# Routed attention and a SoLU expert: six early exponentials stored in the place of w_in, a new sharing of the first casts and marks, a later first v load, and a new order of the early work

## The chip, the cores and the metric

The kernel runs on one core of a Trainium2 chip. A core has five instruction queues that run side by side: TensorE (PE, matrix multiplication, with its weight loads shown apart as PEld), VectorE (DVE), ScalarE (ACT), GpSimd (POOL) and SyncE (SP, which here only issues DMA transfers). Data live in SBUF, matmul results in PSUM banks of 512 float32 columns. Each queue runs its instructions in order and waits where one needs something of another queue. The metric is the time of one execution on the device in microseconds; a profile records one execution, with the span from its first to its last instruction.

## What is computed

Sizes: batch 4, 8 heads, 768 tokens, 64 columns per head, 16 cluster centroids per head; model width 512, inner width 1024.

```python
q_n, k_n, c_n = q / (|q| + 1e-6), k / (|k| + 1e-6), centroids / (|centroids| + 1e-6)
q_assign = argmax(q_n @ c_n.T)          # cluster of every query, per head
k_assign = argmax(k_n @ c_n.T)          # cluster of every key
mask = q_assign[:, None] == k_assign[None, :]
scores = where(mask, (q @ k.T) / 8, -1e9)
attn = softmax(scores) @ v
x = attn, heads side by side            # 3072 tokens x 512
h = x @ w_in                            # 3072 x 1024
solu = h * softmax(h)
out = layer_norm(solu) * g_ln @ w_out   # 3072 x 512
```

## The kernel before

**The mask in the matmul.** A head's 64 columns of q and k are extended by 16 rows that hold, for each token, a one at its own cluster (a "mark"; 32 rows where two heads share a transfer). One matmul over 80 or 96 rows then gives the score plus a constant where the clusters agree, and the exponential of the scaled and shifted result is near zero elsewhere. So the tiles `qk` (six of them, used in turn, one per pair of heads) get their first 64 rows from casts and the rest from the marks.

**The stages of one pair of heads.** The names are those of the order strings; a name such as `ca0.0.1.0.1` has batch, pair, 0 for q or 1 for k, head of the pair, and for pair 0 of batch 0 the half of the tokens.

- `ld` loads q and k into `raw`, `lv` loads v into `vf` (L528), both issued by SP, in order. At most eight transfers are in flight, since a transfer uses one of eight semaphores in turn and waits for the one before it there. The first half-loads are issued partly from ScalarE's queue.
- Batch 0 is turned on TensorE (`tp`, L387) into one of three banks of `hreg`, and copied out as float32 `xt` (`xa`, L394) by VectorE or ScalarE. The other batches are turned on VectorE (`xt`, L408).
- `ca` casts a head's half of `xt` to bfloat16 in `qk` (L432 on ScalarE, L434 and L436 elsewhere).
- `cl` multiplies `xt` with the normalised centroids (L451, L446); VectorE turns the result back (`tb`, L460), takes the largest of each 16 (`mx`, L473), compares (`oh`, L485 or L479), and turns the marks (`ot`, L495 or L492). `pl` places them in `qk` (L515, or L507 for pairs 1 to 3 of batch 0), `bl` clears 16 rows (L524).
- `S` are the score matmuls (L602) into one of three PSUM banks `sps`; `E` the exponentials on ScalarE (L608) into one of nine SBUF tiles `e`; `V` multiplies them with v and a column of ones (L625; v cast by `cv`, L533); `N` divides by the sum (L637, L650).

Pair 0 of batch 0 works with halves of 384 tokens: its two heads have units 0 to 3 of six score banks each, 128x384. All later units have three banks of 512 columns. An `S` waits for the `E` three banks back, an `E` for the `V` that read the tile nine banks back.

**The expert.** `li` and `lo` load w_in and w_out, `wi` casts w_in into `w_in_sb` (L553), `su`, `sk`, `me`, `ce` take the mean out of w_out (L575 to L588). For each of 24 token tiles x is turned by a DMA (`tx`, L680), then `h` (L711), its maximum `hm` (L717), exponential `ex` (L723), product `u` (L730), turned by a DMA (`tu`, L735), statistics `bn`, `ag`, `at`, `al`, the second product `y` (L775), scaling `sc` (L790 or L792) and output `ou` (L802).

**What sets the order.** Everything is added to a list with what it needs, and five strings `ORDER`, written out by hand or by a search, give each engine's queue by these short names with counts (`S2 tp` is two score banks and one turn). `AWAY` names the operations that run on another engine than the usual one. `wm` and `fl` are idle matmuls at the start (L820). Before the loads of w_in are cast, part of `w_in_sb` holds the identity's index (`idx_i`, the first 256 of its first 1024 columns) and the normalised centroids (`c_n`, 256 columns of the second 1024).

Of the kernel before, what the change touches and what calls it, by code (L numbers as in the profile page):

```python
# [22 lines left out]
class Weave:  # L23
# [6 lines left out]
        ld4 lv si ld4 lv lg ld4 lv2 ld4 lo2 ld4 lo ld3 lo ld3 li4 tx ld3 lv3 tx ld4 tu ld9 lv ld tu  # L30
        tx ld3 tu ld3 ou ld2 ou ld tu ld12 tu ld4 lv ld2 ou tx ld3 tu ou ld2 tx lv ld tu ld4 tx ld
        tu ou2 ld lv ld4 tu ld4 tu ld ou ld7 pl ou ld lv2 ld3 tu lv tx ou tu lv pl ld4 ou2 tx lv tu
        tx ou tu pl2 tu2 tx tu tx ou2 tx ou tu tx2 ou tu2 ou2 tu2 ou6
    """
    ORDER["POOL"] = """
        po z ca2 pl2 cv z bl pl2 ca z ca pl2 ca z2 ca3 cv ca cv ca pl3 sg ca cv2 pl3 ca2 gs pl ca cv
        ca wi ca pl2 wi3 bl ca pl2 cv at cv pl ca pl al bl at cv ca pl ca pl cv ca3 al at ca al ca
        at ca pl2 bl cv pl2 ca4 at ca2 al ca pl2 bl pl2 cv2 ca3 al at pl2 bl pl2 ca pl al ca3 at cv
        at pl ca pl2 ca2 pl al cv2 bl cv2 pl2 ca pl al pl at al at pl2 ca3 at al bl cv pl2 bl cv2
        ca3 pl5 al cv3 at al ca2 cv ca cv ca2 at ca2 pl ca al pl2 at2 pl3 at ca cv al at2 al2 at2 al  # L40
        at al3 at al2 at2 al2
    """
    ORDER["PE"] = """
        wm tp2 cp tp cl tp fl5 cl fl4 S3 tp2 S2 tp S cq S tp S2 tp2 S2 V3 S cl S tp2 V3 S gt S tp S
        tp S2 cl S2 V2 S V S2 tp S2 tp S2 V2 S V S2 cl S2 V2 S V2 S3 V S2 V2 S2 V S cl S3 su S2 V3 S
        V S3 V3 S2 V S su S2 V S V3 S3 me S3 V4 S3 cl S3 V4 S2 h S h S2 h S h S2 V3 S2 V h S h V S V
        S h S V S V S h S2 V3 S2 V h S2 h V2 S y3 S2 h3 S3 y V3 h V S2 V2 S cl S3 h2 S2 V3 S y2 S V
        h2 S V y2 S h S V h S2 h S y3 S2 y V3 h S3 cl V2 S V S y S2 y2 S3 V3 S y S2 V3 S2 cl S V S2
        V2 S h S2 V2 S V S h S2 V2 cl V2 S3 y2 S V S2 V y S2 y V2 S3 h2 S V h S h S2 V h S V S V y2
        S h V y2 S2 V S h3 S cl V S2 V2 S h V cl S3 h2 V y V S3 y2 V S h V3 S y S h S2 h2 S3 V2 y h  # L50
        S V S2 y V3 y S3 h3 y S3 V3 S h S V S V cl S V S h S cl V2 S3 y V2 S y S2 y V2 S3 h y V S3 V
        h V2 S3 cl S2 V2 S y3 S2 y S V3 S V S y S2 V S V3 S2 y2 S3 y V2 S2 h V2 S3 h3 S V S2 V y S V
        h2 V2 S y S2 y V y S h2 S3 cl h V S2 V3 S h V2 S3 h2 S y S2 V h S2 V y2 V4 S3 y h S2 h V h V
        S V S y2 S3 V3 h2 S2 h2 S2 y2 S V S h2 S V3 S2 h S h S2 V S y V2 S V y2 S2 h2 S2 h2 V2 S2 V2
        y S2 h V2 h V S2 h S V h S3 V2 h y S V y3 V h3 S2 y3 S2 y h2 V2 h y h y3 h V h V y4 h ptx h
        y4 h2 y3 h2 y ptu2 y6 ptu y ptu y5
    """
    ORDER["DVE"] = """
        cn cb xa ca tb mx oh ot pl2 tb mx oh ot xa3 bl cf cv xa zo xa2 tb ca mx oh gk N ot tb pl mx
        xa2 oh xa cv N ot tb pl N xt mx xt N oh ot tb pl2 ca N pl xt mx N sk oh N ot xt ce3 N tb ce5  # L60
        N hm mx N u oh ot bn N bn ag hm xt2 u N bn2 hm ag sc xt u N bn tb hm mx bn oh ag u xt bn ot
# [6 lines left out]
    """  # L68
    ORDER["ACT"] = """
        wa xa2 ca2 xa ca2 E12 xa2 E6 xa E58 ex E12 ex E8 ex E8 ex E3 sc E5 ca E2 ex E25 ex E9 sc E6  # L70
        ex E5 sc E2 ex E9 ex E8 ex E9 sc E6 ex E18 ex E21 ex E5 sc E3 ex E9 ex E7 sc E2 ex E7 ex E8
        ex E7 ex E6 sc E ex E2 sc E3 ex E2 sc ex sc ex sc ex tu sc tu2 sc2 oz
    """
    AWAY = {}
# [95 lines left out]
def kernel(  # L170
# [11 lines left out]
    nc = tc.nc  # L182
# [1078 lines left out]
```

## Time and profile before

| what | value |
|---|---|
| median of 3 runs (lowest, highest) | 225.04 us (224.11, 225.15) |
| the profiled execution's own time | 223.91 us |
| its span | 221.9 us |
| TensorE busy | 213.1 us (96%) |
| VectorE busy | 197.2 us (89%) |
| ScalarE busy | 191.7 us (86%) |
| GpSimd busy | 127.1 us (57%) |
| granted TensorE clock | 1.00 |

How to read the lines: the first numbers of a timeline row are the start and the length in microseconds, then come the engine, the line of the kernel, the operation, its output and input tiles, their shapes and how many instructions are merged; in brackets stands the idle time of the engine just before, and what released it. SPq and ACTq are the queues that issue DMAs. A row of a table of stretches gives the stretch, its length, and for each engine the busy time and the number of instructions, then the granted clock, the busy share of the DMA engines and GB/s. A row of grouped lines gives busy time and mean nanoseconds, then the idle time before. A row of transfers ends with the microseconds from issue to landing. "a/b/c" are shortest, median and longest. TensorE's busy time is modelled and says little about small rests.

### The profile page before, as it was taken

The page shows a single profiled execution, that of the slowest core. Times are in us where ns is not written, and L with a number is a line of the kernel's source. Part 1 is how long each engine was busy: PE and PEld are TensorE (multiplying, and loading weights), DVE is VectorE, ACT ScalarE, POOL GpSimd, SP SyncE. Part 2 cuts the span into 40 slices and gives each one's busy share as a digit, 9 for nine tenths or more (in the row PEclk, how much of TensorE's full clock was granted, in tenths as well). Part 3 has the DMA queues.
Part 4 walks back from the last instruction along what each step waited for, and adds up shares of the span by engine and source line. Part 5 has one row for each costly group of instructions (what it writes and reads, how often), then busy time and mean ns, then how long its engine had stood idle before and what let it go on. Part 6 is the DMA issues. An engine that isn't in the chain of part 4 may idle for free.

```text
span 221.9 us, 6576 instructions
## 1 busy us (share of the span) xinstructions
PE 213.1 (96%) x2388; PEld 146.3 (66%) x2420; DVE 197.2 (89%) x359; ACT 191.7 (86%) x372; POOL 127.1 (57%) x247
## 2 busy tenths in 40 slices
PE   7899999999999999999999999999999999999994
PEld 2575656677667678776577666777677777755452
DVE  3899898899999999999998999887999889888982
ACT  3689999999899999998889899999899998983363
POOL 3499842954794999547668534953895403022331
PEclk9999999999999999999999999999999999999999
DMA  6997999999897989899999898499930524396723
GB/s 150 337 324 157 244 226 296 277 237 161 141 214 134 218 140 168 193 193 173 187 240 150 153 184 207 90 171 240 227 74 11 97 57 135 85 136 166 177 80 142
DMA packets 125679, 38.80 MB, mean 175 GB/s; under 512 B 115016, under 2 KB 121168, under 8 KB 125648
## 3 DMA queue, kind: packets, MB, share of 16 engines
q1 hardware_dynamic: 123904, 37.87, 80.4%
q10 hardware_dynamic: 1744, 0.52, 1.0%
q8 instruction: 19, 0.31, 0.6%
q14 instruction: 12, 0.10, 0.1%
HBM read 23.11 MB, written 6.29 MB: 132 GB/s over the span
## 4 chain that ended last, share of the span: by engine, by line
PE 83%; ACT 6%; issue 3%; DVE 2%; DMA 2%; POOL 1%; SPq 1%; ACTq 0%; DVEq 0%; POOLq 0%
PE sps L602 27%; PE hreg L711 17%; PE yps L775 17%; PE ops L625 13%; ACT e L608 5%; PE csc L451 4%; DMA raw<-in_q_dram 2%; PE hreg L387 1%; PE hreg L575 1%; PE hreg L775 1%; PE csc L446 1%; DVE u L730 1%; SPq L370 0%; PE utp L699 0%; ACT xt L394 0%
## 5 line engine op out<-in xcount | busy, mean ns | idle before, releaser
L608 ACT ACTIVATE e<-sps 128x512 bf16<-128x512 f32 (+1 forms) x294 | 150.7, 601 | 11.6 <-PE sps L602 9.6
L602 PE MATMUL sps<-qk 80*128 80x256 bf16 (+5 forms) x636 | 94.2, 264 | 2.0 <-POOL qk L515 0.7
L602 PEld LDWEIGHTS <-qk 80*128 80x128 bf16 (+1 forms) x636 | 60.3, 121 | 28.3 <-issue 9.2
L625 PEld LDWEIGHTS <-e 128*128 128x128 bf16 x1152 | 49.2, 97 | 12.3 <-issue 1.9
L625 PE MATMUL ops<-v,e 128*128 128x65 bf16 x1152 | 53.5, 193 | 0.1
L711 PE MATMUL hreg<-w_in_sb,xT 128*128 128x512 bf16 x173 | 49.1, 379 | 1.1
L775 PE MATMUL yps<-w_out_c,uT 128*128 128x512 bf16 x171 | 46.6, 379 | 0.6
L730 DVE TENSOR_TENSOR u<-e_sb,hreg 128x1024 bf16<-128x1024 bf16 (+1 forms) x25 | 29.1, 1168 | 4.8 <-ACT e_sb L723 4.5
L515 POOL COPY qk<-oht 32x384 f32<-32x384 f32 (+1 forms) x50 | 24.4, 488 | 15.6 <-DVE oht L495 13.4
L741 DVE BATCH_NORM_STATS2 bs<-u 128x6 f32<-128x512 bf16 x48 | 31.5, 677 | 0.1
L717 DVE TENSOR_REDUCE nmax<-hreg 128x1 f32<-128x1024 f32 x24 | 29.0, 1208 | 2.5 <-PE hreg L711 2.2
L723 ACT ACTIVATE e_sb<-hreg,nmax 128x1024 bf16<-128x1024 f32 x24 | 26.9, 1123 | 4.5 <-DVE nmax L717 4.4
L434 POOL CAST qk<-xt 64x768 bf16<-64x768 f32 (+1 forms) x31 | 25.9, 837 | 4.8 <-DVE xt L394 3.3
L775 PEld LDWEIGHTS <-uT 128*128 128x128 bf16 x200 | 18.2, 97 | 11.7 <-issue 0.3
L757 POOL TENSOR_SCALAR esq<-es,mv 128x1 f32<-128x1 f32 x24 | 8.5, 355 | 28.9 <-DVE mv L745 20.7
L436 POOL TENSOR_SCALAR qk<-xt 64x768 bf16<-64x768 f32 (+1 forms) x28 | 22.8, 815 | 1.7
L711 PEld LDWEIGHTS <-xT 128*128 128x128 bf16 x192 | 16.7, 97 | 9.5 <-DVE u L730 0.6
L408 DVE STREAM_TRANSPOSE xt<-raw 128x768 f32<-128x768 f32 x24 | 22.7, 953 | 0.2 <-DMA w_g<-in_moe_w_out_dram 0.2
L751 POOL TENSOR_SCALAR es<-esum 128x1 f32<-128x1 f32 x24 | 5.3, 222 | 27.5 <-ACT e_sb L723 27.0
L650 DVE TENSOR_TENSOR x<-ops,den 128x256 bf16<-128x256 f32 (+1 forms) x39 | 19.0, 486 | 1.3
L760 POOL TENSOR_TENSOR alpha<-esq,halves 128x1 f32<-128x1 f32 x24 | 13.5, 561 | 2.0
L533 POOL CAST v<-vf 128x384 bf16<-128x384 f32 x27 | 13.5, 516 | 0.9 <-DMA vf<-in_v_dram 0.2
(80 smaller groups left out, 165.6 us busy)
## 6 DMA issues: line engine op xcount, KB each, us to landing
vf<-in_v_dram SPq DMA_DIRECT2D x16, 384.0 KB, 4.7
out_dram<-y SPq DMA_DIRECT2D x23, 256.0 KB, 2.6
raw<-in_q_dram SPq DMA_DIRECT2D x50, 96.0 KB, 3.3
raw<-in_k_dram SPq DMA_DIRECT2D x50, 96.0 KB, 2.9
w_g<-in_moe_w_out_dram SPq DMA_DIRECT2D x4, 512.0 KB, 4.6
w_st<-in_moe_w_in_dram SPq DMA_DIRECT2D x4, 512.0 KB, 5.9
raw<-in_q_dram SPq DMA_DIRECT2D x3, 384.0 KB, 6.2
raw<-in_k_dram SPq DMA_DIRECT2D x3, 384.0 KB, 6.7
```

What stands on the lines that cost most here:

```text
L434: VEC[e].tensor_copy(dst, src)
L436: VEC[e].tensor_scalar(dst, src, scalar1=inv_C, scalar2=1.0, op0=Alu.mult, op1=Alu.mult)
L515: ins = VEC[e].tensor_copy(dst.bitcast(F32), src.bitcast(F32).unsqueeze(1) .to_broadcast([NB, 2, n // 2]))
L602: nc.tensor.matmul(sps_[n, k][:, c0:c0 + w], side(b, h // 2, 1, h % 2, keys)[r], side(b, h // 2, 0, h % 2, slice(s0 * P, s0 * P + w))[r])
L608: nc.scalar.activation(es[n, k][:, :w], sps_[n, k][:, :w], Act.Exp, scale=exp_scale, bias=-exp_scale)
L625: nc.tensor.matmul(opss[g][:, s, :VW], es[n, k][:, c0:c0 + P], v1[slot(b, h // 2)][:, h % 2, kt, :VW], start=(kt == 0), stop=(kt == n_t - 1))
L711: uses(nc.tensor.matmul(hreg[:, at(f, f2)[1], :], xTs[f][:, dc, :], w_in_sb[:, dc, f2 * FF2:(f2 + 1) * FF2], start=(dc == 0), stop=(dc == ...
L717: uses(nc.vector.tensor_reduce(ff[f, "nmax"][:], pair_of(f), axis=AXY, op=Alu.max, negate=True), *both(f))
L723: uses(nc.scalar.activation(ff[f, "e"][:], pair_of(f), Act.Exp, bias=ff[f, "nmax"][:], accum_out=ff[f, "esum"][:]), *both(f))
L730: uses(nc.vector.tensor_tensor(ff[f, "u"][:, at_], ff[f, "e"][:, at_], pair_of(f)[:, at_], op=Alu.mult), *banks)
L741: nc.vector.bn_stats(ff[f, "bs"][:, f2, :], ff[f, "u"][:, f2, :])
L775: ins = nc.tensor.matmul(dst, ff[f, "uT"][:, at(f, f2)[0] * (n_fc // 2) + c, :], w_out_c[:, fc, cols], start=(fc == chunks[0]), stop=(fc = ...
```

## The change

Four things change, all in the part that starts the attention of batch 0, and with them the order strings:

1. The first six exponentials (banks 0 to 5 in the order of work, units 0 and 1) are written into free columns of `w_in_sb`, two in each of the first three groups of 1024 columns. Nine `e` tiles stay, so up to 15 exponentials can wait for their values matmuls. The casts `wi` now need the values of the first group of units, and both turns of the centroids, to be done.
2. The first v is loaded behind q, k of pair 1 and q of pair 2 instead of ahead of pair 1.
3. `AWAY` gives other engines to casts (`ca`), marks (`pl`), turned tiles (`xa`), v casts (`cv`) and some others, mostly in the first pairs; a mark may now run on ScalarE. A score bank of pair 0 needs only those marks of the keys that it reads.
4. The five order strings differ: SP's and the compute engines' from the start on, up to about two thirds of the kernel, after which they are the same. The number of idle matmuls is the same, nine, split 4 and 5.

```diff
     ORDER["SP"] = """
-        ld4 lv si ld4 lv lg ld4 lv2 ld4 lo2 ld4 lo ld3 lo ld3 li4 tx ld3 lv3 tx ld4 tu ld9 lv ld tu
+        ld4 si ld3 lv ld lv lg ld5 lv ld lo ld lv ld3 lo ld2 lo2 ld3 li ld3 li3 tx ld3 lv
+        ld3 tx ld tu ld7 tu lv ld lv ld4 tx tu ld4 ou ld3 ou tu lv ld12 tu ld4 lv ld2 ou tx
...
     ORDER["POOL"] = """
-        po z ca2 pl2 cv z bl pl2 ca z ca pl2 ca z2 ca3 cv ca cv ca pl3 sg ca cv2 pl3 ca2 gs pl ca cv
+        z2 po ca pl ca zo bl ca pl cv pl bl sg cv ca2 cv ca pl2 ca pl cv ca3 cv pl2 gs ca pl
...
     ORDER["PE"] = """
-        wm tp2 cp tp cl tp fl5 cl fl4 S3 tp2 S2 tp S cq S tp S2 tp2 S2 V3 S cl S tp2 V3 S gt S tp S
-        tp S2 cl S2 V2 S V S2 tp S2 tp S2 V2 S V S2 cl S2 V2 S V2 S3 V S2 V2 S2 V S cl S3 su S2 V3 S
+        wm tp cp tp fl4 cl tp2 fl5 tp cl S tp S tp cq S2 tp2 S2 cl S2 tp S tp S2 tp S V2 S2
+        gt V S V2 S2 V S cl S2 V S V S V S tp S2 tp S2 V2 S V S tp S tp S2 V2 S V S V S cl
...
     ORDER["DVE"] = """
-        cn cb xa ca tb mx oh ot pl2 tb mx oh ot xa3 bl cf cv xa zo xa2 tb ca mx oh gk N ot tb pl mx
+        cn xa cb ca3 tb mx oh ot pl2 tb mx ca xa oh cf ot xa pl2 tb xa mx xa oh gk xa ot N
...
     ORDER["ACT"] = """
-        wa xa2 ca2 xa ca2 E12 xa2 E6 xa E58 ex E12 ex E8 ex E8 ex E3 sc E5 ca E2 ex E25 ex E9 sc E6
+        wa xa ca xa2 pl xa ca E2 xa E xa E74 ex E9 ex E11 ex E10 ca E sc E2 ex E5 sc E7 ex
...
     AWAY.update(dict.fromkeys("""
-        ca0.0.0.0.0 ca0.0.0.1.1 ca1.3.1.1 sc23.0 tu22.1 tu23.1 xa0.0.1.0 xa0.2.1.0 xa0.2.1.1
-        xa0.3.0.0
+        ca0.0.0.1.1 ca1.3.0.1 ca2.1.1.0 ca2.2.1.0 pl0.0.0.0.1 sc23.0 tu22.1 tu23.1 xa0.0.0.1
+        xa0.0.1.0 xa0.1.0.0 xa0.1.1.0 xa0.1.1.1
     """.split(), "ACT"))
...
+        elif e == "ACT":
+            ins = nc.scalar.copy(dst, src.unsqueeze(1).to_broadcast([NB, 2, n]))
...
+    n_lent = 6
+    assert all(wide(*nk) <= HALF for nk in BANKS[:n_lent])
...
     def expo(n, k):
         w = wide(n, k)
-        es[n, k] = ep.tile([P, 512], BF16, name="e")
+        i = BANKS.index((n, k))
+        es[n, k] = (w_in_sb[:, i // 2, 2 * P + i % 2 * HALF:2 * P + (i % 2 + 1) * HALF]
+                    if i < n_lent else ep.tile([P, 512], BF16, name="e"))
...
-    load_v(0, 0)
...
-            add(f"lv{t}", "SP", 0.0, -1990, lambda e: None, [], last_ld[-1:], move=1.3)
+            add(f"lv{t}", "SP", 0.5, first - 34, lambda e: load_v(0, 0), [], ["si"], move=1.3)
...
-            hots = [(i, part) for i in (1, 0) for part in range(2)]
+            hots = ([(1, 0), (0, 0), (0, 1), (1, 1)] if half and not hf else
+                    [(i, part) for i in (1, 0) for part in range(2)])
...
             nd |= {f"pl{ts[1 - x]}.{x}.{part}" for x in range(2)
-                   for part in ((hh,) if apart(b, p) else range(2))}
+                   for part in ((hh,) if apart(b, p) else range(2))
+                   if not (halves_of(b, p) and x and kt % 3 == 2 * (1 - part))}
...
-        if i >= ring_e:
+        if i >= ring_e + n_lent:
...
-        add(f"wi{dc}", "POOL", 1.04, 28 + dc, (lambda e, dc=dc: cast_w_in(dc, e)), [f"li{dc}"],
+        add(f"wi{dc}", "POOL", 1.04, 28 + dc, (lambda e, dc=dc: cast_w_in(dc, e)),
+            [f"li{dc}", "cp", "cq"] + [f"V{n}.{j}" for n in GROUPS[0] for j in range(3)],
             also={"DVE": 0.62})
```

124 lines of the change are left out of this document (67 added, 57 removed).

## The prediction

> **What bounds the kernel now.** I read the page first, then the busy time by stretch, ScalarE's timeline, the chain of waits at the opening, and the durations of single lines. The page's first and fourth parts and a table of four stretches:
>
> ```profile
> PE 213.1 (96%) x2388; PEld 146.3 (66%) x2420; DVE 197.2 (89%) x359; ACT 191.7 (86%) x372; POOL 127.1 (57%) x247
> PE 83%; ACT 6%; issue 3%; DVE 2%; DMA 2%; POOL 1%; SPq 1%; ACTq 0%; DVEq 0%; POOLq 0%
> core 0: us, PE busy (x) PEld busy (x) DVE busy (x) ACT busy (x) POOL busy (x), PEclk, DMA share, GB/s
> 10.00:21.98 11.98, 11.69 (x133) 8.33 (x131) 11.44 (x27) 10.85 (x27) 10.77 (x22) 1.00 0.93 255
> 21.98:45.73 23.75, 23.19 (x323) 15.28 (x322) 21.44 (x43) 22.43 (x46) 15.83 (x25) 1.00 1.02 255
> 45.73:150.00 104.27, 102.80 (x1184) 74.10 (x1203) 98.44 (x170) 98.00 (x190) 68.59 (x126) 1.00 0.95 177
> ```
>
> TensorE carries 83% of the chain, and from 45.73 us, where the expert layer begins, it is busy 102.80 of 104.27 us at the full clock: what is won before that point is kept to the end only if TensorE's order there gets no new waits. Before it the pace is set by the exponentials on ScalarE:
>
> ```profile
> 10.04 3.56 ACT L608 ACTIVATE e<-sps 128x384 bf16<-128x384 f32 x9 [1.11 <-PE sps L602]
> 14.30 1.26 ACT L608 ACTIVATE e<-sps 128x384 bf16<-128x384 f32 x3 [0.71 <-PE ops L625]
> 15.94 0.86 ACT L394 COPY xt<-hreg 128x384 f32<-128x384 f32 x2 [0.38 <-PE hreg L387]
> 16.68 2.58 ACT L608 ACTIVATE e<-sps 128x384 bf16<-128x384 f32 x6
> 19.14 0.49 ACT L394 COPY xt<-hreg 128x384 f32<-128x384 f32 x1
> 19.60 5.62 ACT L608 ACTIVATE e<-sps 128x384 bf16<-128x384 f32 x12
> 25.38 5.50 ACT L608 ACTIVATE e<-sps 128x512 bf16<-128x512 f32 x11 [0.16 <-PE sps L602]
> 37.83 6.23 ACT L608 ACTIVATE e<-sps 128x512 bf16<-128x512 f32 x12 [0.37 <-PE sps L602]
> ```
>
> The reader is to see nine exponentials back to back (ten in flight are not possible, the ring has nine tiles), then 0.71 us of nothing until the first values matmuls (L625) free a tile, then 0.38 us for a turned tile of pair 2, then almost no gap: from 16.68 to 45.73 ScalarE hardly stops. The 24 exponentials of pair 0 have 384 columns and end near 19.60 + 6 x 0.395 = 21.97 us (0.395 is 3.56 / 9).
>
> **The change part by part, against the profiled execution** (223.91 us, span 221.9; the median of the runs is 225.04, 1.13 above it, so the sum is carried to the median as a difference).
>
> *First scores.* Today they wait for two marks in a row on GpSimd:
>
> ```profile
> 8.36 0.38 DVE L495 STREAM_TRANSPOSE oht<-oh 128x192 bf16<-128x192 bf16 x1
> 8.77 0.58 DVE L515 COPY qk<-oht 32x192 f32<-32x192 f32 x2
> 8.88 0.75 POOL L515 COPY qk<-oht 32x192 f32<-32x192 f32 x2 [0.77 <-DVE oht L495]
> 9.68 0.65 PE L602 MATMUL sps<-qk 80*128 80x384 bf16 x3 [0.72 <-POOL qk L515]
> 7.88 1.06 ACT L432 ACTIVATE qk<-xt 64x384 bf16<-64x384 f32 x2
> L394 ACT COPY xt<-hreg 128x384 f32<-128x384 f32 x6 | 2.8, 477 | 1.2 <-PE hreg L387 1.2
> ```
>
> The four marks now go to VectorE (2), GpSimd (1) and ScalarE (1), and the first score group needs only three of them. VectorE's chain to the turned marks is as long as before less a copy and a cast taken out from between (they run beside the centroid work); it starts 0.12 us later, since the centroid turn now stands ahead of the key turn on TensorE, and I put the end of the turn at 8.60 instead of 8.74. GpSimd's one mark then ends at 8.74 + 0.37 = 9.11. ScalarE's mark has no row of before; the nearest, half a 1.06 for a cast of 64x384, gives 0.53 (bounds: 0.27, a copy on VectorE, and 0.59, one cast's mean with its wait), so 8.75 + 0.53 = 9.28. First scores at about 9.45, 0.23 earlier. But ScalarE then has a turned tile of pair 1 (0.48) and a cast (0.53) queued before its first exponential: 9.28 + 1.0 less overlap, 10.15. The exponentials begin **0.1 later** (bounds -0.2 to +0.4).
>
> *Six lent tiles and the late v.* With 15 tiles in flight the tenth exponential waits for nothing, so the 0.71 goes. What would be late next is the first values matmul itself, and it is needed only before the sixteenth. The transfers are read one by one, from issue to landing:
>
> ```profile
> 3.58 0.49 SPq L528 DMA_DIRECT2D vf<-in_v_dram  x1
> 4.11 0.47 SPq L375 DMA_DIRECT2D raw<-in_q_dram  x1
> 5.14 0.47 SPq L375 DMA_DIRECT2D raw<-in_q_dram  x1
> vf<-in_v_dram SPq DMA_DIRECT2D x1, 384.0 KB, 4.4
> raw<-in_q_dram SPq DMA_DIRECT2D x1, 384.0 KB, 4.8
> raw<-in_q_dram SPq DMA_DIRECT2D x1, 384.0 KB, 6.2
> ```
>
> All these loads are 384 KB, so moving v behind two and a half pairs hands its landing to the one that follows: q of pair 1 lands at 3.58 + 4.4 = 7.98 (was 8.91), v at 5.14 + 6.2 = 11.34 (was 7.98). q's turn now stands on TensorE ahead of the first scores, at about 8.3: 0.3 of margin. v's casts move to GpSimd behind a whole cast of pair 1 and a mark, 12.3 and 13.6; the values matmuls stand at about 15.0, behind twelve score banks. Hidden, with 0.9 us to spare. SP issues no more than before, only in another order. The casts of w_in wait for the values of pair 0's first half (done near 17); the first is run after 38 us today, so this wait costs nothing unless it moves up by 20.
>
> *Turned tiles and casts.* The 0.38 was ScalarE standing in its queue for two turned tiles of pair 2; these go to VectorE, as does the first of pair 3, and two of pair 1 come in between the first exponentials, where their transposes are done by then. So 0.38 goes, and one copy of 0.48. Half of that last is given back: the copy ran while TensorE did pair 2's cluster matmuls (0.78 us between two score groups) and that hole of about 0.3 has nothing in it now (bounds 0 to 0.48). VectorE is the engine that this loads, busy 11.44 of 11.98 there:
>
> ```profile
> L394 DVE COPY xt<-hreg 128x384 f32<-128x384 f32 x10 | 5.1, 538 | 0.4 <-PE hreg L387 0.4
> L436 DVE TENSOR_SCALAR qk<-xt 64x768 bf16<-64x768 f32 (+1 forms) x3 | 1.5, 495 | 0.0
> ```
>
> Up to the expert stage it gives up four turned tiles, four marks and five others (a clearing of its own, one of a mark's rows, two v casts, a cast) and takes four turned tiles, five casts and five marks. At 0.54, 0.50 and 0.27 to 0.35 each that is about 6 us both ways. No net cost; a bound of 0.5 either way, since these are means of few.
>
> *Sum at the 24th exponential:* +0.1 - 0.71 - 0.38 - 0.48 + 0.3 = **-1.17 us**. From there to 45.73 the exponentials are as many and in the same order; ScalarE's rest there, 23.75 - 22.43 = 1.3 us, stays (bounds: half of it goes, or half as much comes).
>
> *From 45.73 on* some 390 TensorE pieces change their place a little, up to two thirds of the kernel, and then both programs are the same. Pieces are neither added nor taken away, so TensorE's time is unchanged but for waits. ScalarE gets three casts of whole tiles and two output scalings and gives one cast up:
>
> ```profile
> L432 ACT ACTIVATE qk<-xt 64x768 bf16<-64x768 f32 x1 | 0.8, 842 | 0.0
> L790 ACT ACTIVATE y<-yps,alpha 128x512 f32<-128x512 f32 x13 | 9.0, 694 | 5.6 <-PE yps L775 5.4 <-POOL alpha L760 0.2
> sum 70.00, ACT 64.67; mean ACT 9.24
> ```
>
> That is 2 x 0.84 + 2 x 0.69 = 3.1 us more, nearly all of it between 60 and 130 us, where the last row (the sum over that stretch) leaves it 5.3 us of rest. I take 0 (bounds 0 to +1). The new wait is v of batch 1, pair 1, below; I take it as hidden. Total -1.17, so 222.7 for the profiled execution and **223.9** for the median.
>
> **A rule against it.** Neighbours on VectorE and GpSimd:
>
> ```profile
> L515 POOL COPY qk<-oht x6: 336/342/362, 8.9 to 13.8; 32x192 f32<-32x192 f32 x6
> L515 DVE COPY qk<-oht x2: 255/272/290, 8.8 to 9.1; 32x192 f32<-32x192 f32 x2
> L507 DVE COPY qk<-w_out_c x5: 351/354/878, 20.0 to 34.8; 16x384 f32<-16x384 f32 x5
> ```
>
> In the opening GpSimd's mark starts at 8.88 inside VectorE's pair (8.77 to 9.35) and neither is longer than its kind. One of five later marks on VectorE took 878 instead of 354 ns, beside GpSimd work. Copies and casts from SBUF to SBUF on VectorE rise from 12 to 15 before the expert stage. If one in five is held up by 0.52, three more cost 0.3; if all fifteen are, 7.3, of which only what VectorE's 0.5 us of rest doesn't hold would show. The Trainium skill's page "SBUF — State Buffer", section "SBUF: two separate sides", has VectorE's two-port copies and any GpSimd instruction lock a shared port pair for the whole instruction, the other fully blocked. By that rule the opening's marks would follow one another; its trace does not agree, the 878 ns does. By the rule alone each added copy would be caught (GpSimd is busy 90% there): 3 x 0.52 = 1.6, and the time 225.4.
>
> **The rivals.**
>
> *The values matmuls of batch 1, pair 1, wait (slower).* The load of that v goes from ahead of the second x transpose to behind uT of token tile 1, which itself waits for VectorE's u:
>
> ```profile
> 58.02 1.18 DVE L730 TENSOR_TENSOR u<-e_sb,hreg 128x1024 bf16<-128x1024 bf16 x1
> 61.30 1.72 SPq L735 DMA_TRANSPOSE uT<-u  x1
> DMA to landing us min/median/max: 3.6/4.8/6.8
> L533 POOL CAST v<-vf x7: 500/502/510, 47.5 to 86.7; 128x384 bf16<-128x384 f32 x7
> ```
>
> Today u is done at 59.20 and uT issued at 61.30, because SP is still issuing loads; five of these now stand behind it. With h one microsecond and some half a bank earlier I expect u at 57.5, uT issued at 58, v issued at 59.5, landed at 64.3, cast at 65.0. These values matmuls stand 18.9 us of TensorE work after the first h, near 64.4: a wait of 0 to 0.7. If uT is still issued at 61.30, v comes at 63.0 + 4.8, cast 68.5, and TensorE stands for 4.1 us with everything behind it: 223.9 + 4 = **227.9**. It decides once uT is issued after 59.8 (then 2.3 are lost, which turns -1.17 into +1.13). For it: one piece out of place blocks TensorE's whole queue. Against it: SP's queue is shorter by five issues there.
>
> *TensorE, not ScalarE, sets the pace before the expert stage, and part of the gain is only work put off.* Behind the 24th score bank the new order still has three turns of pair 3 to do, today's has one, each
>
> ```profile
> 22.02 0.33 PE hreg L387 x3
> ```
>
> If TensorE is the bound, 2 x 0.33 of the 1.17 is given back: 0.5 stays, **224.5**, no change by the 0.5% (1.13 us) that a measurement of this kernel can tell. For it: TensorE is busy 23.19 of 23.75 us from 21.98 on, though its ends are modelled. Against it: between the chain's ScalarE groups the exponentials have gaps of only 0.16 to 0.37. The port rule's 225.4 is a case of the same kind.
>
> *More than the sum.* TensorE's rests before and after 45.73, 0.56 and 1.47 by the table, are mostly closed by the new order, 1.3 of 2.0 on top of the 1.17: **222.5**. For it: the order changes around both; against it: the page doesn't tell which of them a new place ends.
>
> **How the numbers follow.** Gain kept 0.42 (223.9); more 0.08; lost on the way, with the port rule, 0.27; slower 0.23. 223.9 lies at the bound itself, so I split its case: faster 0.45 in all, same 0.31, slower 0.24 with a few mishaps of the bounds above. The likeliest case's own range is 223.2 to 224.6 (its bounds added as squares); the range for 8 in 10 reaches from 222.4 to 226.6, a slower case cut at half its price.
>
> **What would show it.** Right: no gap before the tenth exponential, the 24th ends near 20.8, the first marks on three engines side by side, the values matmuls not waiting for a v cast, the first h near 45, and everything after the reordered stretch earlier by the same 1.2. Wrong: a gap at the first exponentials for ScalarE's mark, or for q of pair 1; TensorE waiting for a v cast near 64; the first h no earlier though the 24th exponential is; VectorE copies of 0.8 instead of 0.35.

## The result and the profile after

| | before | changed |
|---|---|---|
| median (lowest, highest), 6 runs each | 224.64 us (223.90, 225.15) | 226.81 us (226.55, 227.51) |
| the profiled execution: time, span | 223.91, 221.9 us | 226.57, 224.6 us |

The changed kernel is slower: ratio 1.0104, 95% interval 1.0076 to 1.0132, some 2.3 us. The forecast was 223.9, faster. An execution that took over 1.5% longer than the fastest of its kernel is left out of the medians and ratios, and since "old opening, new rest" and "h6 later" below were profiled in such a one, at a lower granted clock (0.992), no row of theirs is read. The page of the changed kernel, the same two rows as before (busy time by engine, and the chain that ended last):

```profile
PE 216.7 (96%) x2420; PEld 146.4 (65%) x2420; DVE 197.6 (88%) x361; ACT 193.8 (86%) x375; POOL 124.3 (55%) x242
PE 74%; DMA 8%; POOL 7%; DVE 4%; ACT 3%; issue 2%; SPq 0%; POOLq 0%; DVEq 0%; ACTq 0%
```

The work is the same; TensorE has fallen from 83% to 74% of the chain, and transfers have risen from 2% to 8%, GpSimd from 1% to 7%. Something else now holds TensorE up. ScalarE's timeline of the changed kernel shows that it isn't the opening (exponentials that write `w_in_sb` are those in lent tiles):

```profile
8.78 0.51 ACT L521 COPY qk<-oht 32x384 bf16<-32x384 bf16 x1
10.25 0.84 ACT L620 ACTIVATE w_in_sb<-sps 128x384 bf16<-128x384 f32 x2
12.09 1.25 ACT L620 ACTIVATE w_in_sb<-sps 128x384 bf16<-128x384 f32 x3
13.39 4.89 ACT L620 ACTIVATE e<-sps 128x384 bf16<-128x384 f32 x12
18.59 7.81 ACT L620 ACTIVATE e<-sps 128x384 bf16<-128x384 f32 x17 [0.31 <-PE sps L612]
```

There is no gap at the tenth exponential, and the only hole is the forecast 0.31 at 18.59. Matched piece by piece with the order strings, the 24th exponential ends at 20.99 where the kernel before has 22.00. Over the profiled executions of the kernels told of below, one of each, the median is 20.90 with the new opening (12 executions) and 22.13 with the old one (6, one of them with the lent tiles alone): 1.23 us earlier, and still so at the seventieth score bank, behind which the old order starts the first h (its weights are loaded at 44.23 against 45.45). But the expert stage does not begin earlier. TensorE's timeline and the first maximum of h on VectorE, before and after:

```profile
45.13 0.60 PE L602 MATMUL sps<-qk 80*128 80x256 bf16 x4
45.57 0.60 PE L711 MATMUL hreg<-w_in_sb,xT 128*128 128x512 bf16 x2
...
48.38 1.22 DVE L717 TENSOR_REDUCE nmax<-hreg 128x1 f32<-128x1024 f32 x1
```

```profile
44.23 1.36 PE L612 MATMUL sps<-qk 80*128 80x256 bf16 x6
45.43 0.53 PE L637 MATMUL ops<-v,e 128*128 128x65 bf16 x12
45.79 0.38 PE L612 MATMUL sps<-qk 80*128 80x256 bf16 x2
46.01 0.60 PE L723 MATMUL hreg<-w_in_sb,xT 128*128 128x512 bf16 x2
...
48.40 1.22 DVE L729 TENSOR_REDUCE nmax<-hreg 128x1 f32<-128x1024 f32 x1 [0.23 <-PE hreg L723]
```

That is the new order itself. Counted in TensorE's order strings, 73 score banks and 42 values groups stand ahead of the first h where the kernel before has 70 and 40, and they take until 46.01. So the time won is not lost there yet: it went into work that the kernel before does later. Nor could h have begun much earlier, since x and the last of w_in are there only at 45.5 (below).

From there on the two tables of stretches, before first, then changed, show TensorE losing ground (length, then busy time of PE, PEld, DVE, ACT and POOL):

```profile
45.73:62.00 16.27, 15.73 (x172) 11.58 (x174) 15.57 (x27) 15.45 (x32) 9.44 (x19) 1.00 1.00 177
62.00:80.00 18.00, 17.78 (x205) 12.22 (x207) 17.30 (x31) 17.26 (x33) 13.83 (x25) 1.00 0.97 189
80.00:105.00 25.00, 24.78 (x294) 18.36 (x297) 24.23 (x43) 23.66 (x47) 17.49 (x30) 1.00 0.93 175
```

```profile
45.73:62.00 16.27, 16.09 (x177) 11.55 (x174) 15.52 (x25) 15.04 (x30) 10.15 (x19) 1.00 0.83 148
62.00:80.00 18.00, 17.42 (x195) 11.84 (x194) 16.99 (x29) 17.12 (x33) 10.06 (x19) 1.00 1.06 203
80.00:105.00 25.00, 23.70 (x273) 16.49 (x272) 21.50 (x40) 22.60 (x45) 14.16 (x27) 1.00 0.97 174
```

Between 80 and 105 us every engine does less than before, TensorE by 25 weight loads (272 against 297): they wait for each other. TensorE's idle time (the start of each piece less the work ahead of it since the first score bank, each kind of piece at its usual length) is some 0.8 us below that of before at 44 us, level near 70 us, and some 3 us above at 122 us, behind which it stays. It is a count from modelled matmul times, good to about 0.3 us. The single waits of the changed kernel in that stretch (TensorE's, VectorE's, GpSimd's timelines):

```profile
71.82 0.61 PE L787 MATMUL yps<-w_out_c,uT 128*128 128x512 bf16 x2 [0.43 <-DMA uT<-u]
98.39 0.60 PE L723 MATMUL hreg<-w_in_sb,xT 128*128 128x512 bf16 x2 [1.14 <-DMA xT<-x]
...
72.69 0.98 DVE L414 STREAM_TRANSPOSE xt<-raw 128x768 f32<-128x768 f32 x1 [0.87 <-DMA raw<-in_q_dram]
...
95.46 0.51 POOL L541 CAST v<-vf 128x384 bf16<-128x384 f32 x1 [8.03 <-PE yps L787]
```

The kernel before has no such bracket on TensorE between 62 and 105 us.

### The profile page after: what moved, and what is told of

The parts are those of the page before. It is cut to its first block, busy times and chain, and to the rows that moved or that the text cites. A ratio compares the mean times of both kernels' runs of the same rounds, so it can differ in the third digit from the quotient of the medians.

```text
span 224.6 us, 6602 instructions
## 1 busy us (share of the span) xinstructions
PE 216.7 (96%) x2420; PEld 146.4 (65%) x2420; DVE 197.6 (88%) x361; ACT 193.8 (86%) x375; POOL 124.3 (55%) x242
## 4 chain that ended last, share of the span: by engine, by line
PE 74%; DMA 8%; POOL 7%; DVE 4%; ACT 3%; issue 2%; SPq 0%; POOLq 0%; DVEq 0%; ACTq 0%
PE sps L612 23%; PE hreg L723 17%; PE yps L787 16%; PE ops L637 11%; PE csc L457 4%; DMA raw<-in_q_dram 3%; DMA raw<-in_k_dram 2%; POOL qk L440 2%; ACT e L620 2%; DMA xT<-x 2%; DMA uT<-u 2%; POOL qk L442 2%; POOL qk L513 2%; POOL v L541 1%; PE hreg L583 1%
## 5 line engine op out<-in xcount | busy, mean ns | idle before, releaser
L620 ACT ACTIVATE e<-sps 128x512 bf16<-128x512 f32 (+1 forms) x288 | 148.7, 601 | 11.9 <-PE sps L612 8.9
L612 PE MATMUL sps<-qk 80*128 80x256 bf16 (+5 forms) x636 | 98.2, 264 | 0.7
L637 PEld LDWEIGHTS <-e 128*128 128x128 bf16 x1134 | 50.5, 97 | 13.3 <-issue 2.2
L637 PE MATMUL ops<-v,e 128*128 128x65 bf16 x1134 | 55.8, 193 | 0.2 <-ACT e L620 0.2
L723 PE MATMUL hreg<-w_in_sb,xT 128*128 128x512 bf16 x192 | 53.6, 379 | 1.1 <-DMA xT<-x 1.1
L787 PE MATMUL yps<-w_out_c,uT 128*128 128x512 bf16 x184 | 49.9, 379 | 0.6 <-DMA uT<-u 0.4
L440 POOL CAST qk<-xt 64x768 bf16<-64x768 f32 (+1 forms) x26 | 21.4, 825 | 6.4 <-ACT xt L400 3.8
L442 POOL TENSOR_SCALAR qk<-xt 64x768 bf16<-64x768 f32 (+1 forms) x26 | 21.9, 842 | 1.9
L541 POOL CAST v<-vf 128x384 bf16<-128x384 f32 x29 | 15.1, 526 | 13.2 <-PE yps L787 8.0
L802 ACT ACTIVATE y<-yps,alpha 128x512 f32<-128x512 f32 x15 | 10.5, 697 | 5.1 <-PE yps L787 4.9
```

The source lines that it names most:

```text
L440: VEC[e].tensor_copy(dst, src)
L442: VEC[e].tensor_scalar(dst, src, scalar1=inv_C, scalar2=1.0, op0=Alu.mult, op1=Alu.mult)
L612: nc.tensor.matmul(sps_[n, k][:, c0:c0 + w], side(b, h // 2, 1, h % 2, keys)[r], side(b, h // 2, 0, h % 2, slice(s0 * P, s0 * P + w))[r])
L620: nc.scalar.activation(es[n, k][:, :w], sps_[n, k][:, :w], Act.Exp, scale=exp_scale, bias=-exp_scale)
L637: nc.tensor.matmul(opss[g][:, s, :VW], es[n, k][:, c0:c0 + P], v1[slot(b, h // 2)][:, h % 2, kt, :VW], start=(kt == 0), stop=(kt == n_t - 1))
L723: uses(nc.tensor.matmul(hreg[:, at(f, f2)[1], :], xTs[f][:, dc, :], w_in_sb[:, dc, f2 * FF2:(f2 + 1) * FF2], start=(dc == 0), stop=(dc == ...
```

## The experiments

Two questions: where was the 1.2 us of the opening lost, and what lost 2.3 more. Ratios are to the kernel before, run beside each.

**Splices: which half loses.** The order strings were cut at a point in time: every engine keeps one kernel's order up to it and the other's for what is left.

```diff
 # new opening, old rest (ScalarE's string as an example)
-        wa xa ca xa2 pl xa ca E2 xa E xa E74 ex E9 ex E11 ex E10 ca E sc E2 ex E5 sc E7 ex
+        wa xa ca xa2 pl xa ca E2 xa E xa E73 ex E12 ex E8 ex E8 ex E3 sc E5 ca E2 ex E25 ex E9
...
 # old opening, new rest (SP's as an example)
-        ld4 lv si ld4 lv lg ld4 lv2 ld4 lo2 ld4 lo ld3 lo ld3 li4 tx ld3 lv3 tx ld4 tu ld9 lv ld tu
+        ld4 lv si ld4 lv lg ld4 lv2 ld4 lo2 ld4 lo ld3 lo ld3 li4 tx ld3 lv3 tx ld4 tu ld7 tu
...
```

> The changed kernel up to about 45 us (tiles lent, late v, new shares of casts and marks, its orders), and from there on the order and the engines of the kernel before, for all five queues. Theory (the opening's gain is real and lost behind it): TensorE enters the expert stage about 1.0 us earlier, nothing new is waited for behind it, and the time is 1.0 us under the kernel before (ratio 0.9955, bounds 0.993 to 0.998). Rival A (the opening only puts off work that comes due later, such as normalising on VectorE or loads): the loss stays, ratio 1.005 to 1.011. Rival B (VectorE's or TensorE's whole load sets the end, so an earlier start is worth nothing): ratio 1.000 within 0.002.

> The reverse: the kernel before up to about 46 us (nine exponential tiles, early v, its shares and orders), and from there the order and the engines of the changed kernel. Theory: the rest alone carries the loss, TensorE's idle time grows by 3.7 us (from 0.85 us less to 2.84 us more in the traces of the two kernels), so 228.3 where the kernel before takes 224.6, ratio 1.016; somewhat less (1.011) if the later opening lets the waits at y of token tile 2 and h of token tile 6 shrink. Rival A (the opening carries the loss): 1.000. Rival B: 1.010, the same as the changed kernel, since the opening makes no difference.

> The changed kernel up to about 62 us, then the order and engines of the kernel before for what is left. Theory: the idle time of TensorE stands 0.4 us below that of before at 62 us and the loss comes behind it (first y of token tile 2 at 72 us, h of token tile 6 at 98 us), so the gain of that moment is kept: 0.4 to 1.0 us under the kernel before, ratio 0.996 to 0.998. Rival (the loss is prepared before 62 us by loads and casts in another order): ratio 1.003 to 1.010.

> The changed kernel up to about 80 us, then the order and engines of the kernel before. Theory: the wait at the first y of token tile 2 (about 0.8 us of idle time on TensorE at 72 us) is kept, the later one at h of token tile 6 (1.4 us, and some 0.9 around it) goes: 0.6 us over the kernel before, ratio 1.003 (1.000 to 1.005). If the wait at token tile 6 was prepared before 80 us (x of its token tile late because VectorE and the loads lag), it stays: ratio 1.009.

| kernel | median, us | ratio | 95% interval |
|---|---|---|---|
| new opening, old rest | 224.73 | 0.9983 | 0.9959 to 1.0007 |
| old opening, new rest | 228.07 | 1.0123 | 1.0084 to 1.0162 |
| changed to 62 us, old from there | 225.88 | 1.0048 | 1.0020 to 1.0075 |
| changed to 80 us, old from there | 227.79 | 1.0101 | 1.0061 to 1.0141 |

The new rest costs 1.2% with either opening (0.9983 against 1.0104, and 1.0123), as much as the whole change; the new opening alone is worth between nothing and 0.9 us, where 0.9955 was expected. Stretch by stretch with the new opening, keeping the new order to 62 us takes 0.65% back from the first row, keeping it to 80 us another 0.5%, and putting the old order back behind 80 us wins nothing that the interval can tell. The theory on record for the last row, 1.003, fell; the other reading on record, 1.009, fits: the wait at 98 us (1.14 us in the row above) is prepared before 80 us, or is paid in another form when the order is changed there. The trace doesn't tell which: it has 0.34 us there, but this execution (225.71) lies 2 us under the three others of that kernel (227.75 to 227.89).

**The parts of the rest.** TensorE's new order cannot stand with the old one of the compute engines, since each would wait for the other, so the rest was split in two, and one stretch was tried alone:

```diff
 # SP alone: ORDER["SP"] of the kernel before, from 46 us on
-...tu ld9 lv ld tu tx ld3 tu...
+...tu ld7 tu lv ld lv ld4 tx tu...
 # all but SP: ORDER["PE"], ["DVE"], ["ACT"], ["POOL"] and AWAY from 46 us on are the changed kernel's
 # 46 to 62 us alone: the same four, only the pieces that the changed kernel starts by 62 us
```

> The kernel before with SP's order of the changed kernel from 46 us on, all else as before: v of the pairs (1,1) and (1,2) and a piece of q of batch 2 are loaded later, x of token tile 2 earlier or later by a few issues. Theory (the rest loses by the new places of work on TensorE and the compute engines, the loads only follow): ratio 1.000 to 1.003. Rival (the transfers' order loses it): 1.007 to 1.012.

> The kernel before with the changed kernel's order on TensorE, VectorE, ScalarE and GpSimd from 46 us on and its engines for the casts and scalings there, but SP's order as before. (TensorE's new order can't stand with the old one of the others: each waits for the other.) Theory: nearly all of the 1.2% of the reverse experiment, 1.008 to 1.014. Rival: 1.000 to 1.003, if the loads' order is the cause.

> The kernel before with the changed kernel's order on TensorE, VectorE, ScalarE and GpSimd between 46 and 62 us alone; ahead of it, behind it, and on SP throughout, the order of before. Theory (the loss grows over the whole stretch to 105 us): about a third of the 1.0% that all of the new rest costs, ratio 1.003 (1.001 to 1.005). Rival (it is lost by 62 us): 1.008 to 1.011.

SP alone gave 0.9993 (0.9966 to 1.0019), all but SP 1.0103 (1.0059 to 1.0146), 46 to 62 us alone 1.0022 (0.9994 to 1.0049). The new order of TensorE, VectorE, ScalarE and GpSimd carries the loss; the order of the loads by itself does not. With the old opening most of the loss lies behind 62 us; with the new one over half of it lay ahead of that point (0.65 of 1.2%). So what a stretch costs depends on what stands before it.

**The opening: lent tiles alone.** The kernel before with the six lent tiles and nothing else:

```diff
+    n_lent = 6
...
-        es[n, k] = ep.tile([P, 512], BF16, name="e")
+        i = BANKS.index((n, k))
+        es[n, k] = (w_in_sb[:, i // 2, 2 * P + i % 2 * HALF:2 * P + (i % 2 + 1) * HALF]
+                    if i < n_lent else ep.tile([P, 512], BF16, name="e"))
...
-        if i >= ring_e:
+        if i >= ring_e + n_lent:
...
+            [f"li{dc}", "cp", "cq"] + [f"V{n}.{j}" for n in GROUPS[0] for j in range(3)],
```

> The kernel before with the six lent tiles alone, all orders, engines and loads as before. Theory: the wait of 0.71 us of the tenth exponential goes, the 24th exponential ends 0.7 us earlier, and since h of token tile 0 can start at most 0.6 us earlier than it does (w_in's last cast ends at 44.85), 0.3 to 0.6 us come out at the end: ratio 0.998. Rival A (the whole opening gain needs the new orders; the wait only moves to the next score bank, which stands behind values matmuls in TensorE's queue): ratio 1.000. Rival B (VectorE copies or the late w_in casts get in the way): 1.001 or more.

Measured 1.0013 (0.9993 to 1.0032): rival A. ScalarE's timeline of this kernel:

```profile
10.17 2.40 ACT L612 ACTIVATE w_in_sb<-sps 128x384 bf16<-128x384 f32 x6 [1.11 <-PE sps L604]
12.44 2.73 ACT L612 ACTIVATE e<-sps 128x384 bf16<-128x384 f32 x6
16.06 0.86 ACT L394 COPY xt<-hreg 128x384 f32<-128x384 f32 x2 [0.89 <-PE hreg L387]
```

Twelve exponentials now run without a gap, and the 0.71 us are gone; the next wait, 0.38 us before the change, has become 0.89. Most of the time won is spent at the next piece in TensorE's queue. The lent tiles are worth something only together with the new orders of the opening.

**What stops the opening's gain.** With the old rest, some 0.4 us of the 1.2 are left at the end. Between 30 and 39 us the DMA engines are less busy in the changed kernel. The stretches (last three numbers: clock, share of the DMA engines, GB/s) and x of token tile 0, issue and time to landing; before, then changed:

```profile
30.00:39.00 9.00, 8.85 (x129) 5.43 (x122) 8.12 (x17) 8.25 (x17) 3.07 (x5) 1.00 1.08 287
...
39.60 1.34 SPq L680 DMA_TRANSPOSE xT<-x  x1
...
xT<-x SPq DMA_TRANSPOSE x1, 4.1
```

```profile
30.00:39.00 9.00, 8.78 (x122) 5.54 (x119) 7.84 (x18) 8.25 (x17) 4.97 (x8) 1.00 0.81 180
...
38.71 1.34 SPq L692 DMA_TRANSPOSE xT<-x  x1
...
xT<-x SPq DMA_TRANSPOSE x1, 6.8
...
44.50 1.04 POOL L561 CAST w_in_sb<-w_st 128x1024 bf16<-128x1024 f32 x1 [0.71 <-DMA w_st<-in_moe_w_in_dram]
```

x is issued 0.9 us earlier and lands at 45.5 instead of 43.7, and the last cast of w_in waits for its load. One pair of traces overstates this: over the kernels that load everything, x lands at 43.2 to 46.4 with the new opening (11 traces, median 44.9) and at 43.5 to 45.4 with the old one (5, median 43.7). Three kernels test whether it matters. One issues w_in's loads together, as before; two leave 1.5 MB of w_out out, with the old kernel and with the new opening.

```diff
 # w_in up: SP's order of the changed kernel from the first w_in load on is the old one
-ld3 li ld3 li3 tx
+ld6 li4 tx
 # less w_out
-        nc.sync.dma_start(out=w_g[:, 2 * f2:2 * f2 + 2, :], in_=w_out_r[:, 2 * f2:2 * f2 + 2, :])
+        if f2 == 0:
+            nc.sync.dma_start(out=w_g[:, 0:2, :], in_=w_out_r[:, 0:2, :])
...
-w_g[:, fc, :]
+w_g[:, fc % 2, :]
```

> The changed kernel's opening with the order of before from 45 us on, as in the first experiment, but SP issues the three last pieces of k of batch 1, pair 1 ahead of the first w_in load and the four w_in loads together, as the kernel before does, and the two v loads behind them where that has them. Theory (what the opening wins is stopped at the first h, because w_in's last piece lands at 44.4 and x of token tile 0 at 45.5 in the changed kernel, 42.7 and 43.7 in the kernel before): w_in lands by 43, the first h starts at 44.9 or earlier, and the gain of about 1.0 us is kept: ratio 0.995 (0.993 to 0.997), against 0.998 for the first experiment. Rival (the order of these loads doesn't matter, the load rate or VectorE does): ratio 0.998 again.

> The kernel before with 1.5 MB less to load: the first two of the eight blocks of w_out stand for all eight (so the second product uses wrong weights; all else is computed as before). It is the base of the next one. The four w_in loads and x of token tile 0 then land 2 to 4 us earlier. Theory (in the kernel before the first h waits for little: x lands at 43.7, w_in's last cast ends at 44.85, h starts at 45.46 behind the 24th and later exponentials): at most 0.5 us under the kernel before, ratio 0.998 to 1.000. Rival (the loads set its start too): 0.994.

> The new opening with the old rest and w_in's loads together, as in the experiment of that name, with the same 1.5 MB less to load. Theory (the opening wins 1.1 us up to the exponentials of 45 us and loses them at the first h, which waits for x of token tile 0 that lands at 45.2 to 46.4 in all traces with the new opening): without these loads h starts at 45.0 or earlier, and the time is 0.8 to 1.1 us under that of the kernel before with the same loads left out, ratio to the kernel before 0.994 to 0.996. Rival (the gain is lost to something else than the landing, VectorE or the order behind 45 us): the same time as that kernel, ratio 0.998 to 1.000.

| kernel | median, us | ratio | 95% interval |
|---|---|---|---|
| new opening, old rest, w_in up | 225.18 | 1.0030 | 0.9999 to 1.0062 |
| old, less w_out | 224.53 | 0.9999 | 0.9972 to 1.0027 |
| new opening, old rest, w_in up, less w_out | 223.66 | 0.9961 | 0.9934 to 0.9988 |

The new place of w_in's loads is not the cause: putting them together as before won nothing, and in that kernel's trace x of token tile 0 still lands at 45.85. Leaving 1.5 MB out, and with it three issues of SP, is worth nothing to the old opening and 1.5 us to the new one (225.18 to 223.66), and only then is the new opening clearly faster than the kernel before. Against the new opening with w_in's loads apart (0.9983) the intervals overlap.

The first h, where the expectations for the new opening put the loss, hardly shows it. Without the 1.5 MB x lands at 42.4, yet h starts at 45.99 and u of that tile ends at 52.21; with all the loads these are 45.90 and 52.23. That the first exponential came 0.35 us later in the one trace (10.45 against 10.10) hides no more than that. In this order, too, two more score banks and one more values group stand ahead of the first h than in the kernel before. The difference comes with the next transfer, that of u of token tile 0 (uT). SP's timeline, the transfer's time to landing and TensorE's timeline, with all the loads and then without the 1.5 MB:

```profile
49.94 3.79 SPq L403 DMA_DIRECT2D raw<-in_k_dram  x3
53.83 1.24 SPq L744 DMA_TRANSPOSE uT<-u  x1
...
uT<-u SPq DMA_TRANSPOSE x1, 4.9
...
58.76 1.47 PE L784 MATMUL yps<-w_out_c,uT 128*128 128x512 bf16 x6 [0.84 <-DMA uT<-u]
61.05 1.25 PE L720 MATMUL hreg<-w_in_sb,xT 128*128 128x512 bf16 x5 [0.39 <-DVE u L739]
```

```profile
46.06 4.41 SPq L403 DMA_DIRECT2D raw<-in_k_dram  x3
52.24 1.24 SPq L745 DMA_TRANSPOSE uT<-u  x1
...
uT<-u SPq DMA_TRANSPOSE x1, 3.2
...
57.73 1.46 PE L785 MATMUL yps<-w_out_c,uT 128*128 128x512 bf16 x6
```

With all the loads SP is still issuing loads of k when u is done, so uT goes out 1.6 us later, takes 1.7 us longer, and TensorE waits for it; without them this wait is gone. Whether the bytes or the issues matter was not tried apart. What makes the DMA engines idle between 30 and 39 us is open: single issues of SP take 1.5 to 2.5 us there in the changed kernel and 1.4 us before, in place of 0.5, and no wait is shown for them. The limit of eight transfers in flight doesn't explain the longest (30.46 us, 2.52 long): the transfer eight issues ahead of it, issued at 21.64, landed 6.0 us later. And the profiled executions of the two kernels with less load (223.95 new opening, 224.05 old) hardly differ, so where the 0.9 us between their medians (12 runs each) come from, these two traces don't show. The sentence on record that x lands at 45.2 to 46.4 in all traces with the new opening does not hold, as the range above shows.

**Single waits of the rest.** If one wait were the cause, taking it away should give its time back.

```diff
 # load ahead of uT (SP, names of pieces)
-ld2.0.0.2 tx4 tu2 ld2.0.0 ld2.0.1.0
+ld2.0.0.2 ld2.0.0 tx4 tu2 ld2.0.1.0
 # load and u2 ahead: that, and on VectorE
-xt1.3.0 tb1.2 N12 mx1.2 u2 oh1.2
+xt1.3.0 u2 tb1.2 N12 mx1.2 oh1.2
 # two casts off VectorE: AWAY
-ca1.2.0.0 (DVE)
-cv1.3.1 (DVE)
 # h6 later (TensorE)
-S45.2 h6.0.0 S46.0 h6.0.1 h6.1.0 S46.1 V44.0 V44.1 S46.2
+S45.2 S46.0 S46.1 V44.0 V44.1 h6.0.0 h6.0.1 h6.1.0 S46.2
 # all four edits: all of these, and on VectorE N17 ahead of oh2.0
 # v cast behind marks: h6 later, and on GpSimd
-cv2.0.0 ca2.0.1.0 pl2.0.1.0 pl2.0.1.1 at4 pl2.0.0.0 at5 pl2.0.0.1
+ca2.0.1.0 pl2.0.1.0 pl2.0.1.1 at4 pl2.0.0.0 at5 pl2.0.0.1 cv2.0.0
 # all but normalising, and v cast: all of these without N17
```

> The changed kernel with one transfer moved on SP: the last piece of q of batch 2, pair 0 is issued ahead of x and u of the token tiles 4 and 2 instead of behind them (in the changed kernel SP stood for u until 67.6 us with this load behind it, issued it at 69.9, and VectorE stood 0.87 us for it before 72.7). Theory (between 56 and 100 us VectorE paces the rest, so what it stands there comes out at the end): 0.7 us under the changed kernel, ratio to the kernel before 1.007 where the changed one has 1.0104. Rival (the end is set by TensorE's order and the waits at h of token tile 6, and VectorE catches up): ratio 1.010.

> The same, and on VectorE u of token tile 2 moved up over three pieces of routing and normalising (tb, N, mx), which is where the kernel before has it. Theory: u2 ends 1.6 us earlier, its transposed copy lands ahead of the first y of token tile 2, the 0.6 us of TensorE there go and VectorE no longer stands for the load: 1.0 to 1.5 us under the changed kernel, ratio 1.004 to 1.006. Rival (these two waits are symptoms, and the same time is lost at h of token tile 6 or after it): ratio 1.009 to 1.010.

> The changed kernel with two casts (one of q of batch 1, pair 2, one of v of batch 1, pair 3; 0.87 and 0.39 us on VectorE near 62 and 81 us) back on GpSimd, which stands idle for 1.5 us near 63. Theory A (VectorE paces 56 to 100 us): up to 1.2 us less, ratio 1.005 to 1.007 against 1.0104. Theory B (many small waits on TensorE, each with another cause): 1.009 to 1.011.

> The changed kernel with three pieces of h of token tile 6 placed behind two score banks and three values groups more on TensorE (some 0.8 us of work), so that x of that tile has longer to land (TensorE waits 1.4 us for it there). Theory A (VectorE paces): 1.010, the wait only moves. Theory B (the waits are TensorE's own): 0.6 to 0.8 us less, ratio 1.007.

> The changed kernel with the two casts back on GpSimd, h of token tile 6 later, the load of q of batch 2 ahead of uT, u of token tile 2 up on VectorE, and there also the normalising that x of token tile 6 needs ahead of three routing pieces. Theory A and B alike, if these are the causes: 1.002 to 1.005. Rival (the loss lies in the order as a whole, and what is taken from one wait is lost at the next): 1.008 or more.

> The changed kernel with h of token tile 6 later, as in the experiment of that name, and on GpSimd the first v cast of batch 2, pair 0 behind the cast and the four marks of that pair instead of ahead of them (it waits for a load until 95.5 us in the changed kernel's trace, the marks end at 99.6 behind it, and the values matmuls that need it stand at 105). Theory (one blocked queue hides behind the other wait): the marks are ready by 97, TensorE works on score banks while x of token tile 6 lands, and the 1.4 us there go: ratio 1.004 (1.003 to 1.006), against 1.0104 changed and 1.0096 with h later alone. Rival (the loss comes back at the next wait): 1.008 or more.

> The same, with the two casts back on GpSimd, the load of q of batch 2 ahead of uT and u of token tile 2 up on VectorE, but without the earlier normalising, behind which VectorE stood 1.6 us in the run with all edits. Theory: 1.000 to 1.003, the waits between 62 and 80 us go as well. Rival (they come back elsewhere): 1.004 or more, no better than the run before it.

| kernel | median, us | ratio | 95% interval |
|---|---|---|---|
| changed | 226.81 | 1.0104 | 1.0076 to 1.0132 |
| load ahead of uT | 226.97 | 1.0118 | 1.0085 to 1.0151 |
| load and u2 ahead | 226.45 | 1.0099 | 1.0079 to 1.0119 |
| two casts off VectorE | 226.50 | 1.0084 | 1.0059 to 1.0109 |
| h6 later | 227.02 | 1.0096 | 1.0062 to 1.0130 |
| all four edits | 227.45 | 1.0143 | 1.0103 to 1.0183 |
| h6 later, v cast behind the marks | 227.59 | 1.0122 | 1.0069 to 1.0175 |
| all but normalising, and v cast | 226.44 | 1.0074 | 1.0036 to 1.0112 |

No edit gave back what it was meant to. Where one aimed at a wait, that wait went or shrank, and in most of them another stood elsewhere, with another releaser. TensorE's timelines of five of these kernels between 62 and 105 us, in the order load ahead; load and u2 ahead; two casts off VectorE; all four edits; v cast behind the marks:

```profile
72.34 0.61 PE L786 MATMUL yps<-w_out_c,uT 128*128 128x512 bf16 x2 [0.96 <-DMA uT<-u]
99.12 0.38 PE L611 MATMUL sps<-qk 80*128 80x256 bf16 x2 [0.89 <-POOL qk L522]
```

```profile
66.11 0.38 PE L786 MATMUL yps<-w_out_c,uT 128*128 128x512 bf16 x1 [0.78 <-DVE cst L465]
98.61 0.38 PE L611 MATMUL sps<-qk 80*128 80x256 bf16 x2 [0.55 <-POOL qk L522]
```

```profile
97.70 0.61 PE L722 MATMUL hreg<-w_in_sb,xT 128*128 128x512 bf16 x2 [1.05 <-ACT e L619]
101.81 0.60 PE L786 MATMUL yps<-w_out_c,uT 128*128 128x512 bf16 x2 [0.74 <-DMA uT<-u]
```

```profile
94.57 0.59 PE L786 MATMUL yps<-w_out_c,uT 128*128 128x512 bf16 x2 [1.78 <-DVE mv L756]
```

```profile
103.04 0.60 PE L786 MATMUL yps<-w_out_c,uT 128*128 128x512 bf16 x2 [2.17 <-DMA uT<-u]
```

Moving the load ahead of uT made uT later, and y waited 0.96 instead of 0.43. Moving u up made the routing piece behind it late (0.78 for cst). The normalising moved ahead of routing stood on VectorE for TensorE's values, and u's statistics behind it came late (1.78 for mv). With h later and the marks early, TensorE worked on through 98 us and then stood 2.17 for the next uT. In the last kernel of the table no wait on TensorE between 62 and 105 us is longer than 0.29 us (its idle time at 101 us is some 0.8 us below that of the changed kernel), and of its twelve runs half lie near 225.4 and half near 227.2; what divides them isn't shown. So the theories on record for these runs, that VectorE sets the pace or that single waits of TensorE are the loss, fall as they were stated, and six of the seven kernels fit the rival that what is taken from one wait is lost at the next. The seventh leaves it open: the rival expected it to be no better than "h6 later, v cast behind the marks", and it is 0.5% better, with intervals that overlap; in the faster half of its runs about half of the loss is gone. Which pieces of the new order must go back to end it was not found.

No version that does all of the work clearly beat both kernels: the new opening with the old rest has 0.9983, and its interval takes in no change.

## Why the prediction was wrong, point by point

- *What bounds the kernel.* The condition was stated and right: the gain is kept only if TensorE's order behind 45.73 us gets no new waits. It was then priced at 0.
- *First scores, +0.1 us.* ScalarE's mark took 0.51 (0.53 forecast). In the profiled execution the first exponential started at 10.25 against 10.04, inside the bounds; over the executions above the first score matmul starts at 9.45 against 9.80 and the first exponential at 10.15 against 10.16 (medians). Right within its bounds, but one execution tells little here: the first score matmul starts anywhere from 8.85 to 11.22 with the new opening.
- *Lent tiles and late v, -0.71.* Right in the changed kernel: no gap, v cast at 12.66 and 14.13 (12.3 and 13.6 forecast), values at 15.0. But the 0.71 us belong to the tiles and the order together; the tiles alone give 0.
- *Turned tiles, -0.38, -0.48, +0.3.* The hole of 0.31 us is there. Sum at the 24th exponential: -1.17 forecast, -1.23 as the median of the executions. Right.
- *The port rule.* By the prediction's estimate the rule of the Trainium skill's page "SBUF — State Buffer", section "SBUF: two separate sides", would have cost 1.6 us before the expert stage. The sum there came out without it (-1.23 against -1.17 forecast), so it did not decide here.
- *The values matmuls of batch 1, pair 1.* uT of token tile 1 was issued at 58.90, before the point of 59.8 from which this rival decides, and the v cast ended at 64.70 (65.0 forecast). No wait of TensorE's is shown between 62 and 71 us. The slower side came true, by another mechanism.
- *TensorE sets the pace and some of the gain is work put off.* In part, but not by the turned tiles that this rival counted: the score banks are 1.2 us earlier, the first maximum of h not at all (48.40 against 48.38), since three score banks and two values groups more are done ahead of it.
- *More than the sum.* Not borne out. The 1.47 us of rest that it counted behind 45.73 us are in part missing records: that row has 1184 matmuls for 1203 weight loads.
- **The step that failed: "From 45.73 on ... I take 0 (bounds 0 to +1)".** It was reasoned from TensorE's work being the same. The runs put 1.0% there (2.3 us, 0.6 to 1.5%) for the new order of TensorE and the compute engines alone, with the old opening, and 1.2% with the order of the loads as well; in the changed kernel TensorE's idle time against that of before goes from some 0.8 us less at 44 us to some 3 us more at 122. Which waits of that order make it up stays open. A second, smaller failure is that the gain was carried to the end in full. With the old rest 0.4 us of the 1.17 are left (0 to 0.9): the forecast carried them through the first tiles of the expert stage without asking what these wait for. In the trace of that kernel, the slowest of its twelve runs, the first h waits 0.78 us for the cast of w_in, whose load is late, and a later h, at 61.33 us, 1.19 us for u. Only with 1.5 MB less to load did the new opening end clearly below the old one, by 0.9 us.

## What to carry to other kernels

A gain in the opening is worth only as much as the first pieces of the next stage can use; look up what these wait for, transfers included, and how much work the new order puts ahead of them, before carrying the gain to the end. A new order of hundreds of pieces around the bound engine is a cost of its own, not zero: here it was the largest term. Where every queue is nearly full, taking out the waits that a trace shows one at a time mostly moved them to another releaser; splicing whole stretches of order between the two kernels showed with four kernels which half carries the loss.

## What the runs showed that was not expected

- A lighter load helps the new opening where it doesn't help the old one: 1.5 MB fewer, with w_in's loads together, are worth 1.5 us to the one (225.18 to 223.66) and nothing to the other (0.9999 of the kernel before).
- The DMA engines moved 180 GB/s between 30 and 39 us in the changed kernel against 287 before, with no wait shown for SP's long issues. Over the other traces with all the loads it is 165 to 245 with the new opening and 231 to 275 with the old one.
- Executions differ by a microsecond or two at an equal clock: those of the last kernel above fell into two groups, 224.9 to 226.1 and 226.8 to 227.4 us, at clocks of 0.998 to 1.000, and over the twelve kernels with the new opening the first score matmul started anywhere between 8.85 and 11.22 us. A single trace shows the mechanism, but not its median.
